# An attention and MoE kernel on one Trainium2 core: preparation pieces bound behind unit copies and gates, the first 14 half steps of TensorE's order left to the scheduler, the W34 loads in four buffers of their own

## The chip, the cores and the metric

The kernel runs on one core of a Trainium2 chip. The metric is the device time of one execution in microseconds. Engines are called as in the profile: PE is TensorE (matmuls; PEld its weight loads), DVE is VectorE, ACT is ScalarE, POOL is GpSimd, SP is SyncE, which only issues transfers here.

## The reference

All data is float32.

```
attention: 8 batches, 8 heads, S = 576, D = 64
  scores = q k^T / 8, masked to block_i >= block_j (blocks of 64 positions)
  attn = softmax(scores);  x = attn @ v     -> x of 4608 tokens x 512
first MoE block (dense):  a = x @ w1;  b = x @ w2   (512 x 1024 each)
  x2 = ((a * b) @ w3) @ w_out               (1024 x 1024, 1024 x 512)
second MoE block (routed): logits = x2 @ w_gate (8 experts)
  tokens are assigned to experts greedily by descending logit,
  each expert takes 4608 / 8 = 576 tokens
  out[token] = relu(x2 @ w1[e]) @ w2[e]     for its expert e
```

## The kernel before

Products keep about float32's precision by splitting an operand into a float16 high half and a low half and adding three matmuls (high x high, high x low, low x high). `split` makes the halves: ACT casts the scaled operand (high), DVE subtracts it (low). The scale is a power of two from the largest row sum of squares: `ssq` squares on ACT, `total` adds over the 128 partitions with a matmul against ones and hands the sum to a function `use`. `qk_scale` does this for the two tensors q and k of a group of head pairs, `scale_v` and `prep_v` for v, `prep_w`, `wo_chunk` and `w3_chunk` for the weights. w3 and w_out are multiplied once into W34 (`w34(f)`, eight chunks, stored in DRAM as `w34d`), so that x2 = (a * b) @ W34.

The work before the routed block is laid out over a time in half steps. `at(p, f)` puts function f into a heap at time p, `defer(d, f)` at the present time plus d, and `run(end)` takes them out in order of time and lets them issue their instructions. There are 64 half steps of attention: in each, one part of a head pair's queries goes through S (scores, L283 to L344), `nb` (row maximum on DVE, L301, scaled on ACT, L307), E (exponential on ACT, L309), P (E over its row sum, ACT L325 and DVE L329), a transfer that transposes P to PT, and PV (L383), of which ACT and DVE make `xT`'s two halves (L393, L389). From half step 14 on q and k come packed with their low halves.

Beside it run moe units: 128 units, 16 for each batch, each for one of 8 column groups of w1 and w2 and half of a batch's tokens (288). `moe_unit` issues 12 matmuls for x @ w1 and 12 for x @ w2 into two tiles `ab` of a PSUM pool with two buffers. A time of .15 later the copy `a_sb` (ACT, L421) reads the first, .31 later the gate `g` (DVE, L425) multiplies the second by it. The next unit's w1 group can start when the copy has run, its w2 group when the gate has. Two units stand in each half step, at .26 and .6 of it. Pairs of gates are written to DRAM (`gd`). The last 8 units' gates also feed the logits (`lgp`, L463, copied to `lgT`).

Who sets an engine's order: PE's is as recorded, since `run` stands in `tc.manual_schedule(engines=MS)` with PE in MS. For ACT, DVE and the transfer queues the scheduler of the framework decides, by data dependences, priority in order of recording and its own estimate of time.

After attention, `load_w34` (L1074) reads W34 in four pieces of 512 KB into buffers `g32` and ACT makes the halves (L1077, L1078); POOL adds the tile to the low half with an accumulating transfer. `prep_g` (L1105 to L1110) does the same for a 128-token tile of `gd` in the same two buffers `g32`. `stream` then multiplies the two into x2 (`px`, L1091).

## Time and profile before

| | |
|---|---|
| time, median of 3 runs | 1491.89 us (1490.73 to 1494.48) |
| profiled execution | 1498.06 us, span 1496.4 us |
| PE busy | 1329.2 us, 89% of the span |
| DVE busy | 984.5 us, 66% |
| ACT busy | 929.0 us, 62% |
| POOL busy | 114.2 us, 8% |

The first 14 half steps end at about 182 us, attention at about 777 us; the moe units left over end before 824 us, where `px` begins. Rows of a table by stretches give the stretch and its length, then the busy time and instruction count of PE, PEld, DVE, ACT and POOL, then PE's granted clock as a share of full speed (2.4 GHz), the busy share of the DMA engines and GB/s. Rows of waits give engine, tile and line that stood idle, what it waited for, the sum in us, how often and the longest. Rows of a timeline give start, length, engine, line, instruction, output and input with their shapes, the count of merged instructions, and in brackets the idle time just before, with its releaser.

### The profile page before, as it was taken

Reading aid. Unit: us, or ns where it says so; the run is one execution under the profiler, and the core shown is the slowest. Engines: PE = TensorE matmul, PEld = TensorE weight load, DVE = VectorE, ACT = ScalarE, POOL = GpSimd, SP = SyncE. Lnnn points to the kernel's source line nnn. Section 1 sums busy time; section 2 is a strip of 40 time slices with the busy share of each in tenths; the row PEclk is TensorE's granted clock in tenths of the full one; section 3 lists DMA queues with packets and bytes.
Section 4 is the critical chain, followed back from the end, with each engine's and each line's share of the span. In section 5 each row is a group of like instructions: output and inputs, shape, how many; then the busy total and the mean of one; then the engine's idle time right before and its main releaser. Section 6 shows DMA issues by size and latency. Waiting matters only on the chain. (4 is left out here: it accounts for less than half of the span.)

```text
span 1496.4 us, 31931 instructions
## 1 busy us (share of the span) xinstructions
PE 1329.2 (89%) x12461; PEld 916.2 (61%) x12461; DVE 984.5 (66%) x2914; ACT 929.0 (62%) x2175; POOL 114.2 (8%) x136
## 2 busy tenths in 40 slices
PE   3478888889898897998997999989969999999997
PEld 2355666657676676766765666666656666566663
DVE  6988788687888878778621578777733565454530
ACT  6777686776958678685533355545435667666641
POOL 0000000000000000001001011111022221220011
PEclk9599899999999999999999999999989999999999
DMA  9677789767777757687988898879765867475200
GB/s 273 162 184 182 177 180 202 160 176 143 153 198 161 192 130 181 140 203 180 235 230 203 228 207 211 194 180 218 181 134 115 203 146 193 159 167 154 85 29 35
DMA packets 383815, 257.46 MB, mean 172 GB/s; under 512 B 260784, under 2 KB 344752, under 8 KB 382640
## 3 DMA queue, kind: packets, MB, share of 16 engines
q1 hardware_dynamic: 370464, 213.44, 58.2%
q0 software_dynamic: 11520, 39.87, 12.0%
q8 instruction: 97, 1.59, 0.4%
q10 hardware_dynamic: 1680, 2.11, 0.4%
q14 instruction: 54, 0.44, 0.1%
HBM read 130.84 MB, written 39.86 MB: 114 GB/s over the span
## 5 line engine op out<-in xcount | busy, mean ns | idle before, releaser
L413 PE MATMUL ab<-xT,w1h 128*128 128x288 f16 x1536 | 223.6, 297 | 46.3 <-ACT a_sb L421 39.7
L413 PE MATMUL ab<-xT,w2h 128*128 128x288 f16 x1536 | 217.4, 293 | 9.1 <-DVE g L425 7.3
L413 PEld LDWEIGHTS <-w1h 128*128 128x128 f16 x1536 | 150.5, 102 | 101.2 <-issue 58.2
L1277 PE MATMUL pe<-xT,ewa 128*128 128x288 f16 (+2 forms) x1728 | 192.8, 274 | 2.4 <-ACT xT L1245 0.9
L1295 PE MATMUL pe<-ewb,h 128*128 128x512 f16 (+1 forms) x960 | 189.3, 379 | 0.0
L413 PEld LDWEIGHTS <-w2h 128*128 128x128 f16 x1536 | 154.2, 100 | 55.0 <-issue 11.7
L1277 PEld LDWEIGHTS <-ewa 128*128 128x128 f16 x1728 | 157.3, 99 | 37.0 <-issue 2.0
L329 DVE SCALAR_TENSOR_TENSOR P<-E,rr,P 128x128 f16<-128x128 f32 (+4 forms) x288 | 153.3, 574 | 18.0 <-ACT P L325 17.8
L1295 PEld LDWEIGHTS <-h 128*128 128x128 f16 (+1 forms) x960 | 85.3, 101 | 98.9 <-issue 2.6
L309 ACT ACTIVATE E<-S,nb,cc 128x384 f32<-128x384 f32 (+4 forms) x216 | 136.2, 638 | 1.6
L383 PE MATMUL PV<-PT,v 128*64 128x128 f16 (+1 forms) x2880 | 90.6, 222 | 44.3 <-DMA PT<-P 43.3
L1091 PE MATMUL px<-W34h,gl 128*128 128x512 f32 x288 | 119.8, 416 | 0.7 <-DMA gl<-g 0.7
L1091 PE MATMUL px<-W34h,gh 128*128 128x512 f32 x288 | 120.2, 418 | 0.0
L1091 PE MATMUL px<-W34l,gh 128*128 128x512 f32 x288 | 120.1, 417 | 0.0
L383 PEld LDWEIGHTS <-v 128*64 128x64 f16 x2880 | 80.4, 117 | 60.3 <-issue 31.7
L325 ACT ACTIVATE P<-E,rr 128x512 f16<-128x512 f32 (+3 forms) x176 | 96.1, 600 | 12.9 <-issue 8.3
L301 DVE TENSOR_REDUCE nb<-S 128x2 f32<-128x768 f32 (+3 forms) x128 | 100.9, 814 | 2.2 <-PE S L287 2.0
L1280 DVE SCALAR_TENSOR_TENSOR h<-pe,h 128x288 f16<-128x288 f32 (+2 forms) x144 | 57.9, 420 | 47.2 <-ACT h L1279 46.3
L1298 ACT ACTIVATE y<-pe,s 128x512 f32<-128x512 f32 x36 | 24.7, 687 | 95.0 <-PE pe L1295 65.8
L1235 DVE SCALAR_TENSOR_TENSOR x<-xg,xsc,x 128x512 f16<-128x512 f32 x36 | 27.1, 752 | 84.0 <-ACT x L1234 84.0
L1279 ACT ACTIVATE h<-pe 128x288 f16<-128x288 f32 (+2 forms) x144 | 53.1, 377 | 45.5 <-PE pe L1277 42.8
L1122 ACT ACTIVATE jk<-px 128x512 f16<-128x512 f32 x36 | 21.4, 594 | 86.9 <-issue 68.5
(298 smaller groups left out, 2278.3 us busy)
## 6 DMA issues: line engine op xcount, KB each, us to landing
g<-gd SPq DMA_DIRECT2D x36, 512.0 KB, 5.0
gl<-g POOLq DMA_DIRECT2D x36, 512.0 KB, 5.4
raw<-in_moe_w_dram SPq DMA_DIRECT2D x32, 512.0 KB, 5.1
esa<-in_moe_w_dram SPq DMA_DIRECT2D x8, 2048.0 KB, 10.1
esb<-in_moe_w_dram SPq DMA_DIRECT2D x8, 2048.0 KB, 10.5
gd<-g SPq DMA_DIRECT2D x56, 288.0 KB, 3.7
g<-gd SPq DMA_DIRECT2D x14, 1152.0 KB, 6.9
v<-in_v_dram SPq DMA_DIRECT2D x8, 1280.0 KB, 7.4
```

The costliest lines, as they stand in the source:

```text
L301: nc.vector.tensor_reduce(nb[:, 0, x:x + 2], ps[:, :, o:o + N], axis=AX.X, op=ALU.max)
L309: nc.scalar.activation(d["e"][:, cols[x]], pf_[:, cols[x]], AF.Exp, bias=nb[:, 1, x:x + 1], scale=c[:, 0:1], accum_out=sums[:, x:x + 1])
L325: nc.scalar.activation(hi, d["e"][:, cols[x]], AF.Copy, scale=r[:, 1, x:x + 1])
L329: nc.vector.scalar_tensor_tensor(lo, d["e"][:, cols[x]], r[:, 1, x:x + 1], hi, op0=ALU.mult, op1=ALU.subtract)
L383: nc.tensor.matmul(ps[hh * 64:hh * 64 + 64, c0:c0 + w], vt[:, zv, hh, j, :], s, start=z == 0 and j == 0, stop=z == 2 and j == nj - 1)
L413: nc.tensor.matmul(p[:, :288], w[:, zw, cc, :], x[:, zx, cc, c0:c0 + 288], start=first, stop=cc == 3 and zw == 1)
L1091: nc.tensor.matmul(p, gh[a][:, f], W34[b][:, f], start=f == 0 and a + b == 0, stop=f == 7 and a == 1)
L1235: nc.vector.scalar_tensor_tensor(x16[:, 1], xg[:, :DM], s, x16[:, 0], op0=ALU.mult, op1=ALU.subtract)
L1277: nc.tensor.matmul(p[:, :n], w1[:, a, cc, f * P:(f + 1) * P], t[:, 4 * b + cc, x], start=cc == 0 and a + b == 0, stop=cc == 3 and a == 1)
L1279: nc.scalar.activation(h[:, 0, f, x], p[:, :n], AF.Relu)
L1280: nc.vector.scalar_tensor_tensor(h[:, 1, f, x], p[:, :n], 0.0, h[:, 0, f, x], op0=ALU.max, op1=ALU.subtract)
L1295: nc.tensor.matmul(p[r0:r1], h[:, a, f, k_ * P + r0:k_ * P + r1], EW[e, "b"][0][:, b, f], start=f == 0 and a + b == 0, stop=f == 7 and a == 1)
```

## The change

`spread` chooses for a piece one of two places in a half step, .42 or .76 for ACT pieces and .58 or .92 for DVE pieces, shortly after the unit copies and gates, taking the places in turn by the counts in `taken_`; there the piece is recorded under `tc.issue_after`, which orders it behind the newest unit copy (`newest["a"]`) or gate (`newest["g"]`) on its engine. It is used for squares (`ssq`) and both halves of `split` once the time is past half step 14.3; before that the old way holds. Squares of q and k go to a scratch tile `junk`, and `qkT` is taken only when the scale is known. Several start times move by .1 to 1.25 half steps. `run(HS - .02)`, with HS = 14, stands outside `manual_schedule`, so for these half steps the scheduler orders PE too. The W34 pieces get a pool `tw` of four buffers and are loaded at 66.3, 66.7, 67.1 and 67.5 (its f is 0, 2, 4, 6); their halves and those of the first two `prep_g` are bound behind copies as well.

```diff
--- before.py
+++ after.py
@@ -153,9 +153,38 @@
 
         alone("l", mm)
 
-    def split(hi, lo, x, s, d=.1):
-        nc.scalar.activation(hi, x, AF.Copy, scale=s)
-        defer(d, lambda: nc.vector.scalar_tensor_tensor(lo, x, s, hi, op0=ALU.mult, op1=ALU.subtract))
+    newest, taken_ = {}, {}
+
+    def behind(key, f, *a):
+        with tc.issue_after(newest[key].ins):
+            f(*a)
+
+    def spread(key, p, f, *a):
+        p = max(p, now[0])
+        if p < HS + .3:
+            at(p, f, *a)
+            return
+        places = [x + y for x in range(int(p), int(p) + 3) for y in ((.42, .76), (.58, .92))[key == "g"]]
+        places = [x for x in places if x >= p - 1e-6]
+        places = [x for x in places[:2] if x < p + .6] or places[:1]
+        x = min(places, key=lambda x: taken_.get((key, round(x, 2)), 0))
+        taken_[key, round(x, 2)] = taken_.get((key, round(x, 2)), 0) + 1
+        at(x, behind, key, f, *a)
+
+    def split(hi, lo, x, s, d=.1, p=0, then=None):
+        def low_half():
+            nc.vector.scalar_tensor_tensor(lo, x, s, hi, op0=ALU.mult, op1=ALU.subtract)
+            if then:
+                then()
+
+        def high_half():
+            nc.scalar.activation(hi, x, AF.Copy, scale=s)
+            if now[0] < HS + .3:
+                defer(d, low_half)
+            else:
+                spread("g", now[0] + .1, low_half)
+
+        spread("a", p, high_half)
 
     gate = {}
     qk32, qkT, vhl, xT, PT = {}, {}, {}, {}, {}
@@ -195,8 +224,8 @@
             sv[b] = pow2(sm, m3, "vp")
 
         for x in range(3):
-            defer(.1 * x, sq, x)
-        defer(.9 if b else .5, total, m, .08, use)
+            spread("a", now[0] + .1 * x, sq, x)
+        defer(1.3 if b else .5, total, m, .08, use)
 
     def prep_v(n):
         b, hp = divmod(n, NP)
@@ -220,36 +249,37 @@
 
     pq = {}
 
+    junk = c2.tile([P, 2, S], F16, name="junk", bufs=1)
+
     def qk_scale(g, d0, d1, d2):
         n0, n1 = GROUPS[g]
         w = n1 - n0
 
         def sq(z):
             if z == 0:
-                pq[g] = sm.tile([P, 2], F32, name="qm"), c2.tile([P, 2, 2, 2, S], F16, name="qkT")
-            m, T = pq[g]
-            ssq(qk32[g][:, z, :w], m[:, z:z + 1], T[:, z, 1, :w])
+                pq[g] = sm.tile([P, 2], F32, name="qm")
+            ssq(qk32[g][:, z, :w], pq[g][:, z:z + 1], junk)
             if z:
-                defer(d1, total, m, .08, fin)
+                defer(d1, total, pq[g], .08, fin)
 
         def fin(m2):
-            T = pq[g][1]
+            T = c2.tile([P, 2, 2, 2, S], F16, name="qkT")
             s, e = pow2(sm, m2, "qp")
             c = sm.tile([P, 2], F32, name="cc")
             for z, f in enumerate((1.0, -1.0)):
                 nc.vector.scalar_tensor_tensor(c[:, z:z + 1], e[:, 0:1], f * 0.125, e[:, 1:2],
                                                op0=ALU.mult, op1=ALU.mult)
+            for z in range(2):
+                split(T[:, z, 0, :w], T[:, z, 1, :w], qk32[g][:, z, :w], s[:, z:z + 1], .14,
+                      then=lambda: end(d2))
             pq[g] = s, c, T
-            defer(.05, sp, 0)
-            defer(d2, sp, 1)
-
-        def sp(z):
-            s, c, T = pq[g]
-            split(T[:, z, 0, :w], T[:, z, 1, :w], qk32[g][:, z, :w], s[:, z:z + 1], .14)
-            if z:
-                defer(.15, end)
-
-        def end():
+
+        done = []
+
+        def end(_):
+            done.append(1)
+            if len(done) < 2:
+                return
             s, c, T = pq.pop(g)
             del qk32[g]
             for n in range(n0, n1):
@@ -257,8 +287,12 @@
             if g + 2 < len(GROUPS):
                 load_qk(g + 2)
 
-        sq(0)
-        defer(d0, sq, 1)
+        if g == 5:
+            defer(.02, behind, "a", sq, 0)
+            defer(d0, behind, "a", sq, 1)
+            return
+        spread("a", now[0], sq, 0)
+        spread("a", now[0] + d0, sq, 1)
 
     def last_q(n):
         tq, _, t4, _ = qkT[n]
@@ -418,11 +452,15 @@
                        else lt["p"].tile([P, 2, 288], F32, name="gq", bufs=8))
         t = gg["t"]
         a = mo.tile([P, 288], F32, name="a_sb", bufs=3)
-        defer(.15, lambda: nc.scalar.activation(a, ps["w1"][:, :288], AF.Copy, scale=2.0 ** -15))
+
+        def copy_():
+            newest["a"] = nc.scalar.activation(a, ps["w1"][:, :288], AF.Copy, scale=2.0 ** -15)
+
+        defer(.15, copy_)
 
         def gate_():
             g = t[:, u % 2]
-            nc.vector.scalar_tensor_tensor(g, ps["w2"][:, :288], iv[b][:, f:f + 1], a, op0=ALU.mult, op1=ALU.mult)
+            newest["g"] = nc.vector.scalar_tensor_tensor(g, ps["w2"][:, :288], iv[b][:, f:f + 1], a, op0=ALU.mult, op1=ALU.mult)
             if u % 2:
                 nc.sync.dma_start(gd[f - 1:f + 1, :, b * S + c0:b * S + c0 + 288].rearrange("f p t -> p f t"), t)
             if u >= UL:
@@ -515,7 +553,7 @@
         src = raw.pop(key)
         t = src.rearrange("p (n t) -> p n t", t=2)
         lo, hi = t[:, :, 0], t[:, :, 1]
-        a = stg_w.tile([P, 1024], F32, name="dec2", bufs=1) if key[0] == "w" else stg.tile([P, 512], F32, name="dec")
+        a = stg_w.tile([P, 1024], F32, name="dec2", bufs=1) if key[0] == "w" else stg.tile([P, 512], F32, name="dec", bufs=1)
         nc.scalar.activation(a, hi.bitcast(F32), AF.Abs)
         ai, d = a.bitcast(I32), dst.bitcast(I32)
 
@@ -646,7 +684,7 @@
         def use(m2):
             t = wo["T", f]
             s, e = pow2(sm, m2, "w3p")
-            split(t[:, 0], t[:, 1], w3, s, .12)
+            split(t[:, 0], t[:, 1], w3, s, .12, then=lambda: wo.update({("ok", f): True}))
             fc = sm.tile([P, 2], F32, name="w3f")
             nc.vector.tensor_tensor(out=fc[:, 0:1], in0=e, in1=wo["e"], op=ALU.mult)
             nc.vector.tensor_tensor(out=fc[:, 1:2], in0=e, in1=wo["ee"], op=ALU.mult)
@@ -655,12 +693,13 @@
         def squares():
             m = sm.tile([P, 1], F32, name="w3m")
             wo["T", f] = wo["p3"].tile([P, 2, 1024], F16, name="w3h", bufs=2)
-            ssq(w3, m, wo["T", f][:, 1])
-            defer(.5, total, m, .06, use)
+            spread("a", now[0], ssq, w3, m, wo["T", f][:, 1])
+            defer(.8, total, m, .06, use)
 
         decode(("3", f, h), w3[:, h * 512:h * 512 + 512], squares if h else lambda: None)
 
     def w34(f):
+        assert ("ok", f) in wo
         hold("v")
         t, fc = wo["T", f]
         p = ps_v.tile([P, 512], F32, name="PV")
@@ -762,26 +801,27 @@
             at(8 * b + (4.1 if b < 2 else 4.95), load_v, b + 1)
     for p, g in ((6.1, 2), (8.1, 3), (13.1, 4), (16.1, 5)):
         at(p, load_qk, g)
-    at(14.2, qk_scale, 4, .25, .5, .4)
-    at(16.8, qk_scale, 5, .15, .35, .25)
+    at(14.2, qk_scale, 4, .3, .45, .64)
+    at(16.4, qk_scale, 5, .36, .3, 0)
     for g in range(6, len(GROUPS)):
         b = g // 2 - 1
-        at(8 * b + (8.2 if g % 2 else 6.15), qk_scale, g, .25, .5, .4)
+        at(8 * b + (6.9 if g % 2 else 4.9), qk_scale, g, .3, .6 if g % 2 else .45, 1.02)
     for f in range(8):
         at(2 + .7 * f, prep_w, f)
         at(9.2 + .75 * f, wo_chunk, f)
         at(16.2 + .25 * f, wo_half, f)
         at(18.4 + .5 * f, wo_turn, f)
         at(23.5 + 4 * f, w3_chunk, f, 0)
-        at(24.8 + 4 * f, w3_chunk, f, 1)
-        at(26.42 + 4 * f, alone, "v", w34, f)
+        at(24.9 + 4 * f, w3_chunk, f, 1)
+        at(27.42 + 4 * f, alone, "v", w34, f)
     at(15.8, wo_split)
     at(22.95, wo_gate)
-    at(55.1, late_open)
+    at(55.97, late_open)
     for h in range(UL // 8):
-        at(55.8 + .95 * h, alone, "l", late_run, h)
+        at(56.6 + .9 * h, alone, "l", late_run, h)
 
     MS = {mybir.EngineType.PE}
+    run(HS - .02)
     with tc.manual_schedule(engines=MS):
         run(66.3)
     pa.close()
@@ -1069,8 +1109,11 @@
     gp = pb.enter_context(tc.tile_pool(name="gp", bufs=2, reuse_waits="tile"))
     px = pb.enter_context(tc.tile_pool(name="px", bufs=3, space=PSUM, reuse_waits="tile"))
 
+    es_t = ExitStack()
+    tw = es_t.enter_context(tc.tile_pool(name="tw", bufs=4, reuse_waits="tile"))
+
     def load_w34(f):
-        t = gp.tile([P, 8, P], F32, name="g32").rearrange("p (f a) b -> p f (a b)", f=2)
+        t = tw.tile([P, 2, DM], F32, name="w32")
         nc.sync.dma_start(t, w34d[f:f + 2].rearrange("f p d -> p f d"))
 
         def halves():
@@ -1078,7 +1121,7 @@
             nc.scalar.activation(W34[0][:, f:f + 2], t, AF.Copy)
             nc.gpsimd.dma_start(W34[1][:, f:f + 2].bitcast(F32), t, accum_op=ALU.add)
 
-        defer(.9, halves)
+        defer(1.3, behind, "a", halves)
 
     def stream():
         for j in range(NT):
@@ -1112,7 +1155,7 @@
             gt[j] = gh
 
         if d:
-            defer(d, halves)
+            defer(d, behind, "a", halves)
         else:
             halves()
 
@@ -1180,9 +1223,9 @@
     mats = [(lambda: None, [])] * (2 * E + 3)
 
     for f in range(0, 8, 2):
-        at(66.3 + (0, .6, 1, 1.6)[f // 2], load_w34, f)
-    at(68.2, prep_g, 0, .9)
-    at(68.8, prep_g, 1, .9)
+        at(66.3 + .2 * f, load_w34, f)
+    at(67.9, prep_g, 0, 1.0)
+    at(68.3, prep_g, 1, 1.0)
     with tc.manual_schedule(engines=MS):
         run(70.2)
         for u in range(UL, 126):
@@ -1193,6 +1236,7 @@
         for u in range(126, 128):
             logits(u)
         run(100)
+    es_t.close()
     pm.close()
     rw = pb.enter_context(tc.tile_pool(name="rw", bufs=2, reuse_waits="tile"))
     cwp["pr"] = pb.enter_context(tc.tile_pool(name="pr2", bufs=1, space=PSUM, reuse_waits="tile"))
```

The next two fences are PE's order in the first half steps, before and then changed; `ab_` tiles belong to unit 0 (w1 and w2 of column group 0), S and PV to attention, `v16` is v's halves and PT the transposed P. Before:

```order
L383 MATMUL PV_625<-PT1_563,v16_574 64x128
L146 MATMUL lgp_685<-wm_662,ones_64 128x2
L344 MATMUL S_698<-qk32_147,q4_111 128x512
L344 MATMUL S_698<-qk32_147,q4_111 128x64
L283 MATMUL S_704<-qk32_147 128x512 x2
L287 LDWEIGHTS hide_116
L287 MATMUL S_704<-low_120,hide_116 128x64
L287 LDWEIGHTS hide_116
L287 MATMUL S_704<-low_120,hide_116 128x64
L413 LDWEIGHTS w1h0_72
L413 MATMUL ab_729<-xT_268,w1h0_72 128x288
```

Changed, at unit 0's first matmuls:

```order
L321 MATMUL S_468<-low_120,hide_116 128x64
L447 LDWEIGHTS w1h0_72
L447 MATMUL ab_728<-xT_267,w1h0_72 128x288
L447 LDWEIGHTS w1h0_72
L447 MATMUL ab_728<-xT_267,w1h0_72 128x288
L417 LDWEIGHTS v16_322
L417 MATMUL PV_375<-PT1_319,v16_322 64x128
L417 LDWEIGHTS v16_322
L417 MATMUL PV_375<-PT1_319,v16_322 64x128
L447 LDWEIGHTS w2h0_80
L447 MATMUL ab_741<-xT_267,w2h0_80 128x288
```

Before, unit 0 came after the fourth head pair's PV (PV_625), with its 24 matmuls in a row; now it begins before the second head pair's PV (PV_375), in small pieces between its matmuls, and S_468 of the half step after stands ahead of that PV.

In the steady part, ACT's order around the split of a group of q and k (`qkT` on L157, L181 in the changed kernel; the copies are `a_sb`). Before:

```order
L421 ACTIVATE a_sb<-ab 128x288
L325 ACTIVATE P_122<-E,rr 128x128 x2
L393 ACTIVATE xT<-PV 128x192
L157 ACTIVATE v_6303<-v_124,vp 128x640
L307 ACTIVATE nb<-nb,cc 128x2
L309 ACTIVATE E,sums<-S,nb,cc 128x256 x2
L157 ACTIVATE qkT<-qk_4325,qp 128x1152 x2
L421 ACTIVATE a_sb<-ab 128x288
```

Changed:

```order
L457 ACTIVATE a_sb<-ab 128x288
L343 ACTIVATE E,sums<-S,nb,cc 128x384 x2
L343 ACTIVATE E,sums<-S,nb,cc 128x128 x2
L359 ACTIVATE P_123<-E,rr 128x512 x2
L457 ACTIVATE a_sb<-ab 128x288
L181 ACTIVATE qkT<-qk_4172,qp 128x1152 x2
L359 ACTIVATE P_122<-E,rr 128x128 x2
L427 ACTIVATE xT<-PV 128x192
L457 ACTIVATE a_sb<-ab 128x288
```

The two high halves stood last before a copy; now they stand first behind one.

In the tail, ACT's order over the last units' copies (`W34l`, `W34h`, `gl`, `gh` are the halves of W34 and of `gd` tiles). Before:

```order
L1077 ACTIVATE W34l<-g_12169 128x1024
L1078 ACTIVATE W34h<-g_12169 128x1024
L471 ACTIVATE lgT<-lgp 128x288
L474 ACTIVATE lgx<-lgp 128x64
L421 ACTIVATE a_sb<-ab 128x288
L1109 ACTIVATE gl<-g_12182 128x1024
L1110 ACTIVATE gh<-g_12182 128x1024
L421 ACTIVATE a_sb<-ab 128x288
L1109 ACTIVATE gl<-g_12256 128x1024
L1110 ACTIVATE gh<-g_12256 128x1024
L421 ACTIVATE a_sb<-ab 128x288 x2
```

Changed:

```order
L457 ACTIVATE a_sb<-ab 128x288
L1120 ACTIVATE W34l<-w_12136 128x1024
L1121 ACTIVATE W34h<-w_12136 128x1024
L1152 ACTIVATE gl<-g_12172 128x1024
L1153 ACTIVATE gh<-g_12172 128x1024
L1152 ACTIVATE gl<-g_12218 128x1024
L1153 ACTIVATE gh<-g_12218 128x1024
L457 ACTIVATE a_sb<-ab 128x288 x2
L1152 ACTIVATE gl<-g_12353 128x1024
L1153 ACTIVATE gh<-g_12353 128x1024
L509 ACTIVATE lgT<-lgp 128x288 x2
```

The last W34 pair and the first two `g` pairs stood around three different copies; now all six pieces stand between two copies, and the third `g` pair is ahead of the last two `lgT` in both.

## Rows read from the trace of the kernel before

**Rows 1.** Table by stretches: the first half steps, transition, steady part, tail.

```profile
14.00:182.00 168.00, 112.67 (x1108) 79.22 (x1110) 147.08 (x351) 128.70 (x332) 0.00 (x0) 0.82 0.74 185
182.00:262.00 80.00, 66.56 (x771) 49.79 (x768) 64.62 (x171) 59.34 (x147) 0.00 (x0) 0.92 0.88 194
262.00:700.00 438.00, 397.16 (x4758) 284.64 (x4755) 354.36 (x904) 322.15 (x790) 6.00 (x13) 0.97 0.73 167
777.00:824.00 47.00, 35.73 (x279) 24.98 (x278) 4.44 (x10) 18.10 (x27) 6.32 (x7) 0.89 0.89 219
```

**Rows 2.** Table by stretches: 20 to 50 us.

```profile
20.00:50.00 30.00, 12.33 (x135) 8.96 (x133) 30.00 (x66) 21.95 (x57) 0.00 (x0) 0.69 0.83 201
```

**Rows 3.** Waits of PE, 14 to 182 us.

```profile
PE PV L383 <- DMA PT<-P: 42.7, 15, 9.5
```

**Rows 4.** Waits of PE, 262 to 700 us.

```profile
PE ab L413 <- ACT a_sb L421: 19.2, 10, 2.9
PE ab L413 <- DVE xT L389: 5.5, 4, 4.0
PE lgp L146 <- ACT v L165: 4.7, 4, 1.4
PE ab L413 <- DVE g L425: 4.1, 3, 1.5
PE lgp L146 <- ACT nb L307: 2.9, 1, 2.9
```

**Rows 5.** Timeline of PE in the steady part, four late or slow groups.

```profile
292.00 3.04 PE L413 MATMUL ab<-xT,w1h 128*128 128x288 f16 x12
...
395.36 1.63 PE L413 MATMUL ab<-xT,w1h 128*128 128x288 f16 x12 [1.79 <-ACT a_sb L421]
...
407.24 3.04 PE L413 MATMUL ab<-xT,w1h 128*128 128x288 f16 x12 [2.87 <-ACT a_sb L421]
...
501.22 3.04 PE L413 MATMUL ab<-xT,w2h 128*128 128x288 f16 x12 [1.10 <-DVE g L425]
```

**Rows 6.** Timeline of ACT ahead of the two late copies.

```profile
391.92 1.15 ACT L165 ACTIVATE qkT<-qk 128x1152 f16<-128x1152 f32 x1
...
404.50 2.39 ACT L157 ACTIVATE qkT<-qk,qp 128x1152 f16<-128x1152 f32 x2
406.80 0.40 ACT L421 ACTIVATE a_sb<-ab 128x288 f32<-128x288 f32 x1
```

**Rows 7.** Timeline of DVE, the first low half ahead of the gate.

```profile
406.22 1.41 DVE L158 SCALAR_TENSOR_TENSOR qkT<-qk,qp,qkT 128x1152 f16<-128x1152 f32 x1
```

**Rows 8.** Table by stretches: the slow w1 group of 407 us.

```profile
407.00:410.00 3.00, 2.76 (x12) 1.72 (x12) 3.00 (x7) 2.97 (x11) 0.00 (x0) 0.51 0.81 154
```

**Rows 9.** Waits of PE, 182 to 262 us.

```profile
PE ab L413 <- ACT a_sb L421: 8.4, 5, 2.3
PE S L283 <- DVE qkT L158: 2.4, 1, 2.4
```

**Rows 10.** Waits of DVE, 14 to 182 us.

```profile
DVE rr L313 <- ACT E L309: 8.0, 4, 6.5
```

**Rows 11.** Timeline of PE, the longest stop of the first stretch.

```profile
69.65 0.32 PE L383 MATMUL PV<-PT,v 128*64 128x128 f16 x2 [9.54 <-DMA PT<-P]
```

**Rows 12.** Timeline of ACT in the tail.

```profile
806.69 1.06 ACT L1109 ACTIVATE gl<-g 128x1024 fp32r<-128x1024 f32 x1 [7.63 <-DMA g<-gd]
...
818.88 1.06 ACT L1109 ACTIVATE gl<-g 128x1024 fp32r<-128x1024 f32 x1 [2.77 <-DMA g<-gd]
```

**Rows 13.** Waits of PE, 777 to 824 us.

```profile
PE ab L413 <- ACT a_sb L421: 8.3, 3, 5.7
PE lgp L463 <- ACT lgT L471: 3.0, 1, 3.0
```

**Rows 14.** Timeline of PE in the tail, the late w1 group.

```profile
809.04 3.04 PE L413 MATMUL ab<-xT,w1h 128*128 128x288 f16 x12 [5.69 <-ACT a_sb L421]
```

**Rows 15.** Waits of ACT, 262 to 700 us.

```profile
ACT nb L307 <- DVE nb L301: 33.8, 23, 4.2
```

## The prediction

> **What bounds the kernel now.** I read the table by stretches first. Each row there gives the busy time of TensorE (PE), VectorE (DVE) and ScalarE (ACT) in a stretch, so a row's length less PE's busy time is what PE stood still [rows 1]: 168 - 112.7 = 55.3 us in the first 14 half steps (14 to 182 us), 13.4 in the next 80 us, 438 - 397.2 = 40.8 in the steady part (262 to 700), and 11.3 in the tail (777 to 824), where attention is over and the last moe units run. After 824 us the code is the same apart from places in the ACT order, and I leave that part alone. So PE sets the end nearly everywhere, and it stands about 121 us in these four stretches. The first stretch is the exception: there DVE is busy 147.1 of 168 us, and from 20 to 50 us it is never idle [rows 1, 2]. PE's long waits there, 42.7 us in 15 waits for transposed P tiles [rows 3], are thus waits for DVE, which makes P, and only to a small part for the transfers.
>
> Next I read PE's waits in each stretch. In the steady part 19.2 us in 10 waits are for the ACT copy `a_sb`, 4.1 for the DVE gate `g`, 4.7 for the squares of v and 2.9 for ACT's `nb` scale [rows 4], together 30.9 of the 40.8. Other waits (5.5 for `xT`) aren't touched. The PE rows show the form: the w1 group of a unit starts late by 1.79 or 2.87 us, because the copy that frees its PSUM buffer came late [rows 5]. The ACT rows show why: at 404.50 two high halves of 128x1152 stand ahead of the copy, 2.39 us, and the copy that could have started some 2 us sooner runs at 406.80; thirteen us earlier two squares of 1.15 us stand in a row ahead of the copy, the second at 391.92 [rows 6]. On DVE two low halves of 1.41 us, one of them at 406.22, stand ahead of the gate [rows 7]. After a stop of 2.87 us the w1 group took 3.04 us instead of the 1.63 of its neighbour, and the granted clock in these 3 us was 0.51, the 1.2 GHz level, against a mean of 0.97 in the whole stretch [rows 1, 5, 8]. A stop thus costs up to 1.4 us more than the wait itself.
>
> **The change, part by part.** (1) Pieces bound behind copies and gates, and the new times. Nothing of the work is removed or added: the squares write to another tile, the splits and their low halves are the same instructions. What counts is what stands ahead of a unit's copy in ACT's order. At the place of 404.50 the order of before has E, two high halves, copy; in the changed order both halves stand right behind a copy, followed by one P and one `xT` row before the next copy. Without the 2.39 us the copy at 406.80 would run at 404.4 and PE's stop of 2.87 shrinks to about 0.5. The two squares of 391 us are now one behind each of two copies; the stop of 1.79 was made by two squares, of which only one is left there (1.15 us less), and the other starts right behind the earlier copy, so I expect it gone. On DVE the two low halves now stand behind a gate, but in one pair, so 2.8 us of DVE's work is pushed ahead of the next `nb` reduction, which the exponentials need. That is the cost of this part: not work, but a later S-to-P chain. I take three quarters of the 30.9 us, 23, and of the clock's extra time (five w1 or w2 groups, the first at 292.00 and the last at 501.22 [rows 5], some 6 us together over 1.63 each) about 4: -27. The bounds: all of it and the 5.5 of `xT` too, -38 (the 30.9 + 6 + some), and a half of 36.9, -18, for a DVE that is 81% busy on average (354.4 of 438) [rows 1] and would be 354.4 / 411 = 86% once it is 27 us shorter.
>
> (2) The transition, 182 to 262 us. The same kind of waits, 8.4 for copies and 2.4 for the low half of `qkT` [rows 9], 13.4 in all. Groups 4 and 5 must still be made in few half steps here, and DVE works 64.6 of 80 us; the durations of the trace, summed over the rows that stand between gates 15 and 27 in DVE's order, fall from 64.3 to 59.4 us, since some work comes elsewhere. I take half, -7, within -2 and -13.
>
> (3) First 14 half steps. The scheduler now writes PE's order. By the order, S of a half step stands before the PV group of the half step before it, and unit 0's w1 and w2 matmuls stand one to three at a time between PV's. PE's work isn't changed. What can be won is DVE's idle time: 168 - 147.1 = 21 us, of which 8.0 is waits of the row sums `rr` for E [rows 10], the kind that an earlier S shortens; but 6.5 of that is one wait at the start, before any PV. Against it stands that PE waits in order at each small piece. The nearest row for a lost place is the stop of 9.54 us at 69.65, an ordinary matmul behind a late transpose [rows 11]; one such new stop on the path of S would eat the gain. I take -5; the bounds are -14 (two thirds of DVE's idle time) and +8 (one long stop less a little).
>
> The Trainium skill, page "TensorE: Matmul & The Clock Gate", section "Step-by-step: what each phase is for", says that matmuls stay in program order and only weight loads are pulled ahead. This trace agrees: the whole of PE stood for 9.54 us though other S work was at hand; it speaks against this part of the change, and its result is the second rival below.
>
> (4) Tail. Before, W34 halves and the first `g` pieces share two buffers, so ACT stands 7.6 us at `gl` for a load that could not start before the buffer was free [rows 12], the copy behind it is late, and PE stands 5.69 us for that copy and 3.00 for `lgT` [rows 13, 14], and one more w1 group runs at 3.04 (1.4 us lost) [rows 14]. With the 2.6 of two shorter copy waits that is the 11.3 of [rows 1], and about 2 for the clock, 13 in all. In the changed order the four W34 loads go out together, and every W34 piece stands behind a copy. But two W34 pieces and two `g` pairs, 6 x 1.06 = 6.4 us [rows 12], now stand between two copies, which leaves about 2 us of stop at the last unit; and `lgT` still stands behind the third `g` pair, whose load needs the first's buffer: gl, accumulation, load, gl again took 818.88 - 806.69 = 12.2 us before [rows 12] and moves up by only some 6 us, so some 6 us of stop remain there. 13 - 8 = -5, within -10 (only 3 left) and -1.
>
> The Trainium skill, page "DMA: Bandwidth & Descriptors", section "Issuing engines are not separate DMA queues", says that transfers interleave on the same 16 engines whichever engine issues them. By that rule four loads of 512 KB would land together, 2 MB at the 219 GB/s of this stretch [rows 1] = 9.6 us, instead of one after another; since these loads now have about a half step more time before their first use, the sum stays as it is.
>
> **The sum.** -5 - 7 - 27 - 5 = -44 us. The profiled execution took 1498.06 us (span 1496.4), 6 us above the median of the runs, 1491.89; the gain is taken off the median: 1448.
>
> **Rivals.** (a) DVE becomes the bound of the steady part. For it: the half steps that hold a W34 chunk's decode and split give DVE about 14.8 us in the changed order by the trace's durations, against some 15 for PE, and the low halves in pairs make `nb` late. Against it: 81% on average. Then half of (1) and (2) goes, 17 us: 1465.
> (b) Slower: PE's order in the first stretch. One mechanism: a w1 or w2 piece placed ahead of an S waits for an `xT` that DVE, never idle from 20 to 50 us, makes late; S comes late, so DVE gets its next `nb` late and its idle time grows in each half step. The mean of the PV waits there is 42.7 / 15 = 2.8 us [rows 3]; lost anew in each of 13 half steps that is 37 us, which leaves 1485; it decides from 44 / 13 = 3.4 us per half step on. At 4 us, +52: 1491.89 - 39 + 52 = 1505. Against it: S stands one half step further ahead, so one late piece has some 12 us (168 / 14) of slack.
> (c) Nothing comes of it: the pieces delay E, `nb` and P instead, PE waits at PV and `xT` instead of at w1, and only the tail's 5 us are left: about 1487 to 1492. For it: ACT waits 33.8 us for `nb` already in the steady part [rows 15], so the chain over S, `nb`, E, P isn't far from late.
>
> **How the numbers follow.** Forecast 0.69, (a) 0.17, (b) 0.08, (c) 0.06. The forecast's own range, from its bounds, is 1417 (-75) to 1478 (-13), and as they hardly fall together about 1424 to 1474; with (a) inside and part of (c) left out the range is 1424 to 1480. A difference under 0.3%, 4.5 us, can't be told from none. The forecast and (a) lie beyond it on the fast side, (b) on the slow side; (c) is mostly none: faster 0.87, same 0.05, slower 0.08.
>
> **What would show it.** In the changed profile the steady part should have copy waits of a few us instead of 19.2, gate waits no larger than before, and few 3.04 us groups; the time of S-to-P waits (`PV` for PT, `ab` for `xT`) shows (c) if it grows by as much. DVE at 90% or more there shows (a). Half step 14 (the first S against a packed q) came at 182 us: some 5 us sooner shows (3) right, later (b). In the tail no W34 piece should wait for a load, and the largest stop should be that at `lgT`. The forecast is wrong if the steady part still stands 25 us or more, or the first stretch is longer than 175 us.

## The result and the profile after

The changed kernel takes 1454.31 us (median of 4 runs, 1446.03 to 1458.13) against 1491.31 for the kernel before in the same comparison: a ratio of 0.974, 95% interval 0.970 to 0.979. That is 37 us less where 44 was forecast (1448), and inside the range. The terms of the sum, however, came out less well than the sum. The profiled execution took 1458.13 us, the longest of the four, as the one of the kernel before was above its median too.

To lay the stretches of two kernels side by side I cut both traces at the same pieces of work instead of at the same times: the ends of the gates of units 15, 31, 111 and 119 (counted from 0), and the first and last `px` matmul. In the kernel before these are 176.9, 272.5, 732.1, 775.2 and 822.3 us, in the changed one 164.6, 253.6, 696.9, 736.8 and 780.6. The table by stretches of the changed kernel (columns as in [rows 1]):

```profile
14.00:164.60 150.60, 118.89 (x1154) 77.65 (x1155) 142.07 (x350) 128.78 (x333) 0.00 (x0) 0.94 0.88 207
164.60:253.60 89.00, 75.61 (x882) 55.98 (x882) 72.87 (x187) 64.07 (x161) 0.00 (x0) 0.92 0.81 188
253.60:696.90 443.30, 412.36 (x4986) 296.17 (x4984) 366.76 (x945) 331.24 (x824) 5.98 (x13) 0.98 0.78 177
696.90:736.80 39.90, 39.26 (x495) 27.99 (x494) 17.87 (x38) 18.93 (x46) 0.00 (x0) 1.00 1.02 241
736.80:780.60 43.80, 36.10 (x350) 24.50 (x342) 4.89 (x11) 18.78 (x29) 6.32 (x7) 0.93 0.97 255
780.60:1054.30 273.70, 261.65 (x1871) 179.62 (x1869) 192.67 (x869) 133.97 (x244) 28.38 (x33) 0.98 0.82 198
```

The same cuts in the kernel before:

```profile
14.00:176.90 162.90, 110.50 (x1086) 78.09 (x1087) 143.65 (x344) 125.36 (x324) 0.00 (x0) 0.81 0.73 184
272.50:732.10 459.60, 418.25 (x5007) 299.53 (x5004) 368.92 (x942) 333.77 (x826) 6.00 (x13) 0.97 0.73 171
775.20:822.30 47.10, 35.83 (x325) 24.62 (x320) 4.80 (x12) 18.43 (x28) 6.32 (x7) 0.89 0.89 225
```

The first stretch is 12.3 us shorter, the transition 6.6 (95.6 to 89.0), the steady part 16.3, the one from unit 111 to 119 is 3.2 shorter, the tail 3.3, and the px stretch behind it 2.7 longer (271.0 to 273.7); with 1 us more gained later the two profiled spans differ by 40.0. The moe units are the same work at each cut, attention is not: by unit 15's gate the changed kernel has issued 54 more PV matmuls than before, by unit 31's only 8 more. The first two stretches are therefore best taken together, 272.5 to 253.6, 18.9 us. In the steady part PE's idle time fell from 41.4 to 30.9 us and its busy time by 5.9, in the main the clock's share (granted 0.98 against 0.97; the stretch holds 4986 matmuls against 5007).

PE's waits in the changed kernel, first stretch (two rows) and steady part; the answers to [rows 3] and [rows 4]:

```profile
PE S L317 <- ACT E L343: 15.0, 4, 6.8
PE PV L417 <- DMA PT<-P: 6.8, 7, 2.3
...
PE PV L708 <- DVE xT L423: 8.7, 5, 2.5
PE ab L447 <- DVE g L463: 7.1, 4, 1.8
PE ab L447 <- ACT a_sb L457: 6.6, 10, 1.4
PE ab L447 <- DVE xT L423: 4.3, 5, 1.2
```

Between the same two gates the kernel before has the waits of [rows 4]. The copy waits fell from 19.2 to 6.6 us and the waits for v's squares and `nb` are gone. But a wait is there that the kernel before didn't have: W34's matmuls (L708) wait for the low half of `xT` on DVE, which must have read the one PV buffer. Of its five stops three are 2.46 or 2.47 us, the others 1.15 and 0.15. The timelines of PE and then DVE at one of the three:

```profile
353.34 7.04 PE L708 MATMUL PV<-wo,w3h 128*128 128x512 f16 x24 [2.46 <-DVE xT L423]
...
381.55 1.63 PE L447 MATMUL ab<-xT,w2h 128*128 128x288 f16 x12 [1.81 <-DVE g L463]
```

```profile
346.16 0.52 DVE L463 SCALAR_TENSOR_TENSOR g<-ab,vr,a_sb 128x288 f32<-128x288 f32 x1
346.59 2.74 DVE L176 SCALAR_TENSOR_TENSOR qkT<-qk,qp,qkT 128x1152 f16<-128x1152 f32 x2
...
350.71 0.81 DVE L363 SCALAR_TENSOR_TENSOR P<-E,rr,P 128x576 f16<-128x576 f32 x1
...
352.11 0.79 DVE L303 COPY q<-qkT 64x128 f16<-64x128 f16 x4
352.93 0.36 DVE L423 SCALAR_TENSOR_TENSOR xT<-PV,xT 128x192 f16<-128x192 f32 x1
```

Both low halves of a group stand behind one gate, 2.74 us, and everything after them on DVE is late up to `xT`, at 352.93. PE stops 2.46 us, and the W34 group after the stop takes 7.04 us; behind the two short stops it takes 5.35.

### The profile page after: what moved, and what is told of

It is laid out like the page before. It is cut to its first block, busy times and chain, and to the rows that moved or that the text cites. A ratio compares the mean times of both kernels' runs of the same rounds, so it can differ in the third digit from the quotient of the medians.

```text
span 1456.4 us, 31972 instructions
## 1 busy us (share of the span) xinstructions
PE 1328.6 (91%) x12461; PEld 910.1 (62%) x12461; DVE 977.5 (67%) x2914; ACT 926.3 (64%) x2175; POOL 114.2 (8%) x136
## 5 line engine op out<-in xcount | busy, mean ns | idle before, releaser
L447 PE MATMUL ab<-xT,w1h 128*128 128x288 f16 x1536 | 218.9, 292 | 24.8 <-DVE xT L423 11.7
L359 ACT ACTIVATE P<-E,rr 128x512 f16<-128x512 f32 (+3 forms) x176 | 97.2, 603 | 11.9 <-issue 2.9
L417 PEld LDWEIGHTS <-v 128*64 128x64 f16 x2880 | 76.4, 113 | 27.1 <-issue 18.9
L1342 ACT ACTIVATE y<-pe,s 128x512 f32<-128x512 f32 x36 | 24.7, 687 | 95.0 <-PE pe L1339 65.8
L463 DVE SCALAR_TENSOR_TENSOR g<-ab,vr,a_sb 128x288 f32<-128x288 f32 x112 | 57.6, 514 | 33.0 <-PE ab L447 25.4
```

The costliest lines, as they stand in the source:

```text
L359: nc.scalar.activation(hi, d["e"][:, cols[x]], AF.Copy, scale=r[:, 1, x:x + 1])
L417: nc.tensor.matmul(ps[hh * 64:hh * 64 + 64, c0:c0 + w], vt[:, zv, hh, j, :], s, start=z == 0 and j == 0, stop=z == 2 and j == nj - 1)
L447: nc.tensor.matmul(p[:, :288], w[:, zw, cc, :], x[:, zx, cc, c0:c0 + 288], start=first, stop=cc == 3 and zw == 1)
L463: newest["g"] = nc.vector.scalar_tensor_tensor(g, ps["w2"][:, :288], iv[b][:, f:f + 1], a, op0=ALU.mult, op1=ALU.mult)
```

## The experiments

The runs were timed in three more comparisons, each with the kernel before again. It took 1495.50 us beside the first four runs below; 1494.52 beside the third g buffer, low halves apart, W34 later and low halves unbound; and 1491.01 beside the tail part, both edits and high halves apart. Times of different comparisons can thus differ by some 4 us for that reason alone. The lengths of stretches come from one profile of each run.

**PE's order recorded again.** The changed kernel without part (3).

```diff
-    run(HS - .02)
     with tc.manual_schedule(engines=MS):
+        run(HS - .02)
         run(66.3)
```

> The changed kernel, but PE's order in the first 14 half steps is recorded by hand as before. Theory A (the scheduler's PE order made the first stretch shorter): gate of unit 15 comes 10 to 14 us later than in the changed kernel, near the 176.9 us of before, PE's waits for PT in that stretch go back to some 40 us from 6.8, the time rises by 10 to 22 us to 1465 to 1476. Rival B (the first stretch got shorter by the other parts, the later v totals and the single dec buffer): unit 15's gate stays within 3 us of 164.6 and the time within 4 us of 1454.

1470.81 us: 16.5 above the changed kernel, or 12.3 if each is taken against the kernel before of its own comparison (24.7 us below it here, 37.0 there). Unit 15's gate comes at 179.9 us, 15.3 later, and PE's largest wait is the old one again:

```profile
PE PV L417 <- DMA PT<-P: 29.0, 14, 6.9
```

Theory A, although the gate comes a little later than its 10 to 14 us and the wait stays below its 40. The steady part takes 438.2 us here, 5 less than with part (3). Its idle time is the same (31.1 us against 30.9), with the same 8.7 us of W34 waits; only PE's busy time is less, 407.1 instead of 412.4, at a granted clock of 1.00 instead of 0.98. The last section comes back to this.

**The scheduler's PE order alone.** The kernel before with `run(HS - .02)` ahead of `manual_schedule` and nothing else.

> The kernel before with nothing changed but PE's order in the first 14 half steps left to the scheduler. Theory A: the first stretch alone, 12 us at unit 15 and up to 22 at unit 19, so 1470 to 1480; the steady part (unit 31 to 111) stays at 459.6 us, as its order is that of before. Rival B: no gain without the other parts, 1488 to 1495. Rival C: part of the first stretch's gain is lost in the transition, whose preparation of groups 4 and 5 then comes at the old times: 5 us gained, 1486.

1481.43 us, ratio 0.992 (0.989 to 0.995), 14.1 below the kernel before: theory A, just outside its range. Unit 15's gate is only 2.5 us earlier, but the 13th `xT` of attention 14.9 us (169.1 against 184.0; 164.9 in the changed kernel); from unit 19 on the gain is 14.1, by unit 31 14.2 (258.3 against 272.5), and is kept: the steady part takes 459.7 us and its copy waits 19.1, as before. PE's waits in the first stretch (14 to 174.4 us) show what replaced the 42.7 us of [rows 3]:

```profile
PE S L283 <- ACT E L309: 21.9, 7, 7.3
PE PV L383 <- DMA PT<-P: 5.8, 6, 2.2
```

PE now stands at S for a free score buffer instead of at PV for PT: S is ahead, and PV's operands are there when PE comes to them.

**No binding.** The changed kernel, pieces at their places in time but bound to nothing.

```diff
     def behind(key, f, *a):
-        with tc.issue_after(newest[key].ins):
-            f(*a)
+        f(*a)
```

> The changed kernel, but the pieces are only recorded at their places of the time axis and no longer ordered behind a copy or gate. Theory A (the binding removes the late copies): the steady part (unit 31 to 111, 443.3 us in the changed kernel) gets 10 to 16 us longer and the waits for a_sb return to 15 us or more: 1464 to 1470. Rival B (the places alone do it, since the scheduler follows the order of recording): steady part within 4 us of 443.3, time 1450 to 1458.

1482.95 us. The steady part takes 459.6 us, the length of before: without the binding nothing of its gain is left. It is not the same stretch for that: PE's idle time is 47.2 us instead of 41.4 and its busy time 412.4 instead of 418.3, so with the new times alone PE waited longer. Whether the binding would do as well at the old times was not run. Its waits:

```profile
PE ab L446 <- ACT a_sb L456: 16.8, 16, 4.8
PE ab L446 <- DVE g L462: 13.9, 16, 1.7
```

Theory A. The total is above its 1470, since the tail lost too: 55.2 us from unit 119's gate to px, against 43.8. The next run shows why.

**The W34 buffers alone.** The kernel before with pool `tw` for the W34 loads; old times, no binding.

> The kernel before with nothing changed but the four buffers of the W34 loads (old load times, old halves). Theory A: in the tail the waits of the W34 pieces for their loads go (7.7 us), and the 7.6 us wait at gl shrinks since its buffer is free, so the tail is 5 to 8 us shorter: 1484 to 1487. Rival B: the loads were not what bound the tail, since lgT still stands behind the third g pair: within 2 us of 1491.

1500.58 us, ratio 1.003 (1.0005 to 1.0055): 5.1 us slower, just clear of none. From unit 119's gate to px it takes 53.4 us against 47.1. The W34 waits did go, but with all four tiles there the eight W34 pieces run in one row, and then, on ACT:

```profile
800.84 1.06 ACT L1112 ACTIVATE gl<-g 128x1024 fp32r<-128x1024 f32 x1 [11.86 <-DMA g<-gd]
801.80 0.39 ACT L421 ACTIVATE a_sb<-ab 128x288 f32<-128x288 f32 x1
```

The first `g` piece stands ahead of a unit's copy and holds it for the 11.9 us in which its load isn't there; PE's longest stop at a copy is 11.0 us. Both theories fell: the buffers neither help nor do nothing, they hurt, as long as nothing ties `g`'s halves behind the copies.

**The tail part alone, whole.** The kernel before with the buffers, the later places and the binding of W34's and the first `g` halves.

> The kernel before with the change's tail part alone, now whole: four W34 buffers, the later places, and the W34 and first g halves bound behind unit copies. Theory A (the binding is what makes the four buffers useful; unbound, they moved a wait for the gd load ahead of a copy): from unit 119's gate to px 43 to 45 us instead of 47.1 and 53.5 with the buffers alone, time 2 to 5 us below before. Rival B (the tail's gain in the changed kernel came from the stretch before it): 47 us or more and no gain.

1487.47 us, ratio 0.998 (0.996 to 0.999); 41.5 us from unit 119's gate to px, less than theory A's 43 to 45. Theory A; the small gain is clear of none. Its waits are the two that the forecast named for the tail, some 6 us at `lgT` and 2 at the last unit:

```profile
PE lgp L472 <- ACT lgT L480: 6.3, 1, 6.3
PE ab L419 <- ACT a_sb L428: 2.1, 1, 2.1
```

**A third g buffer.** The changed kernel; the third `gd` tile goes into the W34 pool and is bound behind the last copy.

```diff
-        g = gp.tile([P, 8, P], F32, name="g32")
+        if j == 2:
+            g = tw.tile([P, 2, DM], F32, name="w32").rearrange("p f (a b) -> p (f a) b", b=P)
+        else:
+            g = gp.tile([P, 8, P], F32, name="g32")
...
+        elif j == 2:
+            behind("a", halves)
```

> The changed kernel, where the third tile of gd in the tail is loaded into the W34 loads' pool (its first piece is long free) instead of the first g buffer, its halves bound behind the last copy. Theory A (the 5.0 us stop at lgT is ACT's wait for that load, 5.0 us): that stop goes and px starts 4 to 6 us earlier after unit 119's gate: 39 us instead of 43.8, time 1449. Rival B: the load comes no sooner, since the SP queue issues it behind other waits, and nothing changes: 43.8 us, 1454.

1447.44 us, 38.8 us from unit 119's gate to px: theory A. In the changed kernel ACT waited for that tile, and `lgT` stood behind it:

```profile
776.23 1.06 ACT L1152 ACTIVATE gl<-g 128x1024 fp32r<-128x1024 f32 x1 [5.01 <-DMA g<-gd]
777.19 1.04 ACT L1153 ACTIVATE gh<-g 128x1024 fp32r<-128x1024 f32 x1
778.13 0.39 ACT L509 ACTIVATE lgT<-lgp 128x288 f32<-128x288 f32 x1
```

With the buffer the same piece runs at 771.36 without a wait. The px stretch is 6.1 us shorter too (267.6), which I hadn't expected. A part of it the traces show: in the changed kernel px begins right behind PE's stop at `lgT`, and for its first 4.1 us the granted clock is 0.50, the 1.2 GHz level:

```profile
778.58 2.13 PE L501 MATMUL lgp<-gq,W34g 128*32 128x288 f32 x12 [5.00 <-ACT lgT L509]
...
780.60:784.70 4.10, 4.10 (x12) 3.20 (x11) 0.00 (x0) 0.00 (x0) 0.00 (x0) 0.50 0.41 84
```

With the third buffer that stop is 0.9 us and the granted clock is 1.00 over all of px; PE's busy time there is 257.5 instead of 261.7 us. The rest is idle time, whose cause wasn't followed.

**Low halves apart.** The changed kernel; the two low halves of a q and k group take different places.

```diff
-        places = [x for x in places if x >= p - 1e-6]
+        places = [x for x in places if x >= p - 1e-6 and x not in (used or ())]
...
+        if used is not None:
+            used.append(x)
```

> The changed kernel, with the two low halves of one q and k group never behind the same gate. Theory A (the pair of 2.74 us on DVE is what makes the steady part's new stops: 2.46 us of W34's matmuls for xT and 1.81 of a w2 group for the gate, per batch): both stops fall below 1 us, the W34 group takes 5.35 instead of 7.04 us, units 31 to 111 take 425 to 432 us instead of 443.3, the time is 1438 to 1446. Rival B (DVE is late as a whole, not at one place): the stops move to other gates and xT, units 31 to 111 stay within 4 us of 443, time 1450 to 1458.

1451.75 us (1447.16 to 1453.97): a gain over the changed kernel that these times can't tell from none. The steady part is 437.5 us, 5.8 shorter (3.3 of it idle time), between the two theories. The W34 stops fall to 0.64 at most (8.7 to 3.7 us in all) and the gate stops from 7.1 to 0.3, as theory A said, but copies and `xT` give 7.9 of these 11.8 us back, as rival B said:

```profile
PE ab L450 <- ACT a_sb L460: 10.3, 13, 1.4
PE ab L450 <- DVE xT L426: 8.5, 9, 2.1
PE PV L711 <- DVE xT L426: 3.7, 6, 0.6
```

**W34 later.** The changed kernel with `w34` at 27.68 + 4f.

> The changed kernel, with W34's matmuls a quarter half step later (27.68 + 4f instead of 27.42 + 4f), so that they stand behind the half step's four unit groups instead of before two of them. Theory A: the 2.46 us stop and the slow W34 group after it (7.04 against 5.35) go, as xT's low half has run by then: 3 to 4 us for each of 5 chunks, units 31 to 111 take 426 to 433 us, time 1438 to 1444. Rival B: the stop only moves to the PV group behind, which now stands right after W34 and waits for the ACT copy of its result out of the one PV buffer, 1 to 2 us per chunk: units 31 to 111 take 434 to 440.

1456.99 us; the steady part takes 448.7 us, 5.4 longer. The W34 stop went, but gate stops rose to 13.8 us in 11 waits. The place of W34's matmuls was the place where DVE's lateness showed, not its cause. Both theories fell.

**Low halves unbound.** The changed kernel; ACT's pieces stay bound, all low halves on DVE (those of q and k, and of v and w3) are recorded soon after their high halves as before.

```diff
         def high_half():
             nc.scalar.activation(hi, x, AF.Copy, scale=s)
-            if now[0] < HS + .3:
-                defer(d, low_half)
-            else:
-                spread("g", now[0] + .1, low_half)
+            defer(d, low_half)
```

> The changed kernel, with the low halves on DVE recorded .1 to .14 after their high halves and bound to no gate; the ACT pieces stay bound. Theory A (ACT's binding carries the gain, DVE's low halves follow their high halves anyway): units 31 to 111 within 4 us of 443.3 and the time within 4 of 1454. Rival B (DVE's binding matters too): gate waits rise from 7.1 to over 12 us, units 31 to 111 take 450 us or more, 1461 or more.

1441.75 us, ratio 0.965 (0.961 to 0.968): both theories were wrong, the binding on DVE was a loss. The steady part takes 430.5 us, 12.8 less than the changed kernel and 29.1 less than before. DVE at the place shown above, and PE's W34 group:

```profile
342.28 1.42 DVE L176 SCALAR_TENSOR_TENSOR qkT<-qk,qp,qkT 128x1152 f16<-128x1152 f32 x1
...
345.60 0.51 DVE L460 SCALAR_TENSOR_TENSOR g<-ab,vr,a_sb 128x288 f32<-128x288 f32 x1
346.02 1.41 DVE L176 SCALAR_TENSOR_TENSOR qkT<-qk,qp,qkT 128x1152 f16<-128x1152 f32 x1
...
349.55 0.35 DVE L420 SCALAR_TENSOR_TENSOR xT<-PV,xT 128x192 f16<-128x192 f32 x1
```

```profile
PE PV L705 <- DVE xT L420: 2.1, 4, 0.6
PE ab L444 <- DVE g L460: 7.0, 4, 1.8
PE ab L444 <- ACT a_sb L454: 5.1, 10, 1.4
```

One low half now runs a gate earlier (342.28), and `xT` follows 3.4 us sooner (349.55 against 352.93, in a trace that is 1.6 us ahead at unit 47's gate). From the gate before it, `xT` starts after 3.95 us instead of 6.77. Of these 2.8 us the low half is about 1.3; the rest is a `P` piece and the copies of `q`, which stood ahead of `xT` in the changed kernel and now follow it. Of the 12.8 us, PE's idle time gave 7.5 (30.9 to 23.4) and its busy time 5.3 (412.4 to 407.1); three W34 groups of 5.35 instead of 7.04 us are 5.1 of that.

**Both edits that helped.** Low halves unbound and the third g buffer.

> The changed kernel with both edits that helped: low halves on DVE bound to no gate, and the tail's third gd tile in the W34 loads' pool. Theory A (they act in different stretches and add up): 12 to 13 us from units 31 to 111 and 5 us from the tail, time 1435 to 1439 against 1454. Rival B (the tail's gain needs the slack that the steady part had): only one of the two, 1441 to 1449.

1430.64 us (1428.84 to 1433.07), ratio 0.960 (0.958 to 0.961) to before: better than both kernels, and by more than theory A. The steady part takes 430.4 us, the tail 38.5, px 267.0 instead of 273.7, a gain in px like that of the run with the third buffer, which theory A had left out.

**High halves apart too.** The same, with a group's two high halves never behind the same copy.

> The kernel of the run before it, with the two high halves of a q and k group never behind the same copy, so that their low halves come apart too without being bound. Theory A (the gate stop of 1.81 us per batch is left by the pair of low halves at the one place where they still stand together): that stop goes, 4 x 1.8 us, units 31 to 111 take 422 to 425 instead of 430.5 us, time 1428 to 1433. Rival B (the second high half, a third of a half step later, makes its low half and the next head pair's S late): a stop of S for qkT or of the w2 group for the gate of 1 us or more per batch takes its place, 1434 to 1440.

1436.63 us: 6 us worse. The gate stop is gone, but S now waits 5.0 us for E and the steady part takes 437.8 us, of whose 7.4 us more 3.4 are idle time: rival B by its time, with E where it had `qkT` and the gate.

```profile
PE ab L447 <- ACT a_sb L457: 6.3, 11, 1.4
PE ab L447 <- DVE xT L423: 5.4, 5, 2.3
PE S L317 <- ACT E L343: 5.0, 4, 1.5
```

## Why the prediction was right, and where not

**(1), steady part: -27 forecast, 16.3 measured, outside the term's own bounds (18 to 38).** The mechanism was right as far as it went: late copies were the stops, and binding removes them. Its waits for copies, v's squares and `nb` fell by 20.2 us; with the gates', which rose by 3.0, the waits that the term aimed at are 17.2 us less, of the 23 that I took. But the forecast named as a sign of being wrong that PE stands 25 us or more in the steady part, and it stands 30.9. The step that failed is the one on DVE, "a later S-to-P chain", which I let three quarters of the gain survive. That chain did get later, ACT's waits for `nb` rose from 36.3 to 58.6 us, but the run with unbound low halves keeps 57.2 of them and is 12.8 us shorter, and S waits for E only 0.7: it wasn't what cost. What DVE made late is the low half of `xT`, and with it the PV buffer that W34 needs, 8.7 us, a resource that wasn't on my list; and gates, whose waits grew from 4.1 to 7.1 us where my list of signs had them no larger. Unbound, the low halves leave 29.1 us of gain, so binding them cost 12.8. Keeping the two low halves of a group apart gives 5.8 of it back; what the other 7.0 are, the bound place itself or the low halves of v and w3, which that run left bound, is not shown. Rival (a), half of the gain lost to DVE, is nearest to what happened in this part, but not by DVE being full: DVE is busy 366.8 of 443.3 us, 83%; it is late at a few places. The clock's part, 4 forecast, came out near the 5.9 us of busy time, though its list of five slow groups, the last at 501 us, missed two of 3.08 and 2.95 us at 691 and 694 us.

**(2), transition, and (3), first half steps: -7 and -5 forecast, 6.6 and 12.3 measured between the cuts.** Taken so, both look inside their bounds. The runs divide the 18.9 us by unit 31's gate otherwise: part (3) alone gives 14.2, and taking it away from the changed kernel costs 17.6 (271.2 against 253.6), which leaves 1.3 to 4.7 us for all the other parts. Term (3) was thus too small by 9 to 13 us and outside its bound of 14, and term (2) too large by 2 to 6: its copy waits fell (8.4 to 2.5 us), but a wait of 5.2 for `xT` and one of 3.5 for squares came in their place. That (2) seems to fit to 0.4 us is luck.

The mechanism of (3) was right in its direction and mis-sized: DVE's idle time in the first stretch fell from 19.2 to 8.5 us, more than the 5 that I took. I looked for gain in the 8.0 us of [rows 10], and those waits are still 7.5; it came from PE no longer standing in order at PV (42.7 us in [rows 3], 39.8 of them before unit 15's gate, to 6.8). The sign that I named, the first S against a packed q, did not come at 182 us in the kernel before, which was a misreading, but at 204.88; the second row is the changed kernel, 21.3 us sooner:

```profile
204.88 0.66 PE L283 MATMUL S<-qkT 64*128 64x384 f16 x6
183.58 0.66 PE L317 MATMUL S<-qkT 64*128 64x384 f16 x6
```

Rival (b)'s late pieces exist, a w1 piece waits up to 2.2 us for `xT`, but S is far enough ahead that attention isn't held. (Its 1485 us keeps the 5 us that the rival takes away; without them it is 1490.) The rule that matmuls stay in program order, from the Trainium skill's page "TensorE: Matmul & The Clock Gate", section "Step-by-step: what each phase is for", agrees with both profiles; here it worked for the change, since the better program order is what took PE's waits at PV away.

**(4), tail: -5 forecast, 3.3 measured, and 2.7 given back in the px stretch.** The stops that I said would remain, 6 us at `lgT` and 2 at the last unit, measured 5.0 and 2.1, and right behind the first of them PE runs at the 1.2 GHz level, px's first 4.1 us included. That four buffers are worth something only together with the binding was not in my sum: alone they made the tail 6 us longer. No W34 piece waited for its load in the changed kernel, so what the transfers cost each other, the rule that I cited from the Trainium skill's page "DMA: Bandwidth & Descriptors", section "Issuing engines are not separate DMA queues", changed nothing that these rows show.

The total came out near by luck: a term too large by 11 us and one too large by 2 to 6 met one too small by 9 to 13, and 3 us between units 111 and 119 that nobody had counted.

## What to carry to other kernels

Binding a long piece behind the instruction that frees a buffer is worth as much as the waits it removes, but each engine needs its own check: with ACT's pieces bound and DVE's free the steady part took 430.5 us, with both bound 443.3, with none bound 459.6. On DVE the bound pieces pushed back what frees another buffer. Before pieces are bound to a place, list every single-buffered tile whose reader stands behind them. And buffers that let transfers come early also let their consumers come early in an in-order engine: free the buffer and fix the consumer's place together.

## What the runs showed of the hardware

A stop of PE can cost more than its length. In the changed kernel each of the three stops of some 2.46 us ahead of a W34 group is followed by a group of 7.04 instead of 5.35 us, 1.7 us more; in the stretch of the first such group, 353 to 361 us, the granted clock was 0.79:

```profile
353.00:361.00 8.00, 7.66 (x44) 3.46 (x45) 6.48 (x16) 5.52 (x12) 0.00 (x0) 0.79 1.04 273
```

But it need not. With PE's order recorded again the same three stops stand ahead of the same groups, and only one group is slow (granted clock 0.78 in it, 1.00 in the two others):

```profile
371.04 5.35 PE L708 MATMUL PV<-wo,w3h 128*128 128x512 f16 x24 [2.46 <-DVE xT L423]
...
458.43 6.85 PE L708 MATMUL PV<-wo,w3h 128*128 128x512 f16 x24 [2.47 <-DVE xT L423]
...
547.31 5.35 PE L708 MATMUL PV<-wo,w3h 128*128 128x512 f16 x24 [2.46 <-DVE xT L423]
```

The kernel before shows it too. Of its four stops of 2.87 us for a copy in the steady part one is followed by a w1 group of 3.04 us [rows 5], one by 2.00, and two by the full-speed 1.63:

```profile
316.64 1.63 PE L413 MATMUL ab<-xT,w1h 128*128 128x288 f16 x12 [2.87 <-ACT a_sb L421]
...
589.13 1.63 PE L413 MATMUL ab<-xT,w1h 128*128 128x288 f16 x12 [2.87 <-ACT a_sb L421]
```

So the length of a stop alone doesn't tell what comes behind it: here 0 to 1.7 us. PE's busy time in the steady part doesn't follow its idle time either: 418.3 us busy with 41.4 idle in the kernel before, 412.4 with 30.9 in the changed one, 412.4 with 47.2 without the binding, 407.1 with 31.1 with PE's order recorded, and 407.1 with 23.4 with unbound low halves. A difference of some 5 us between two versions can be the clock's alone, and has to be parted from idle time before a cause is named.
